# A_wo matmuls in a hardware loop with register addresses, the PE program not aligned to a block, filler matmuls written out

## Chip, cores, metric

One core of one Trainium2 chip (trn2). The metric is device time in microseconds (us), lower is better. The kernel is one decode step: an attention over a window of a key and value cache and a small gated feed-forward block, added up for a single token.

## The reference

```python
def reference(A_x, A_k_cache, A_v_cache, A_wq, A_wo, B_x, B_w_r, B_w_gate, B_w_up, B_w_down):
    x = A_x                                   # (1, 1, 512)
    xn = _layernorm(x)
    # A: 32 query heads on 8 key/value heads, the last 4096 places of the cache
    q = xn @ wq; p = softmax(q k^T / sqrt(128)); o = p v
    a = o.reshape(1, 1, 4096) @ wo            # A_wo: (4096, 512), bf16, 4 MB
    # B: one token, so it always is the chosen one
    y = (silu(xn @ w_gate) * (xn @ w_up)) @ w_down * sigmoid(xn @ w_r)
    return x + a + xn + y
```

(This is cut and put together from two functions; names as in the original.) All of it has to be read once: 30.7 MB of weights and cache for some 40 million multiply-adds. What matters here is the product with A_wo, (1 x 4096) by (4096 x 512): 32 matmuls with a contraction of 128 each.

## The kernel before

Every weight is loaded by one DMA queue in the order of use. A_wo comes in four transfers of 1 MB, one for 8 matmuls each, and w_down in five small ones behind it:

```python
    wo_chunks = [(0, 8), (8, 16), (16, 24), (24, 32)]
    t_wo = [dma(sy, f"wo{k}", wo_sb[:, j0 * D:j1 * D], wo_v[:, j0 * D:j1 * D]) for k, (j0, j1) in enumerate(wo_chunks)]
    wd_chunks = [(0, 4), (4, 8), (8, 11), (11, 13), (13, 14)]
```

The end of the program of TensorE (PE), all into one row of PSUM:

```python
    te.matmul(a_ps, lhsT=zst[:, 0:1], rhs=zmov[:], start=True, stop=False, skip_group_check=True)
    fill(F4)
    PE.need(t_oT2)
    for k, (j0, j1) in enumerate(wo_chunks):
        PE.need(t_wo[k])                      # wait for this quarter of A_wo
        for j in range(j0, j1):               # a Python loop: 32 matmuls written out
            te.matmul(a_ps, lhsT=oT2[:, j:j + 1], rhs=wo_sb[:, j * D:(j + 1) * D], start=False, stop=False, ...)
    PE.need(t_hT)
    for k, (j0, j1) in enumerate(wd_chunks):
        PE.need(t_wd[k])
        for j in range(j0, j1):
            ins = te.matmul(a_ps, lhsT=hTr[:, j, 0:1], rhs=wd_sb[:, j * D:(j + 1) * D], ...)
    ...                                       # + residual on VectorE (DVE), then the write of 1 KB
```

`fill(n)` emits a hardware loop of n passes with two matmuls of zeros; it keeps PE busy while it waits (L150 from 65.36 to 66.17 us, just ahead of A_wo). Hardware loops (`te.Fori`) also drive the keys (8 passes, 40 matmuls each) and the values (8 passes). A line at the start of PE's program, `te.addr_align(256, offset=0, max_nops=0)`, asks for a start at a multiple of 256 instructions; such a stretch is called a block below. In the records of the kernel before, a branch over the padding stands at 1.05 us (295 ns), and the instruction packets have 16 KB. How many instructions one packet holds is not shown.

Of the kernel before, what the change touches and what calls it, by code (L numbers as in the profile page):

```python
# [38 lines left out]
def kernel(  # L39
# [16 lines left out]
    D = A_x.shape[2]  # L56
# [10 lines left out]
    RJ = (HQ * DH) // P  # L67
# [30 lines left out]
    zst = sb("zst", [P, P], BF16)  # L98
    zmov = sb("zmov", [P, 512], BF16)
# [16 lines left out]
    oT2 = sb("oT2", [P, RJ], BF16)  # L116
# [8 lines left out]
    ps = nc.alloc_psum_tensor("ps", [P, 8, 512], F32)  # L125
# [6 lines left out]
    a_ps = ps[0:1, 5, :]  # L132
# [5 lines left out]
    wo_sb = k_flat[:, FB * D:(FB + RJ) * D]  # L138

    S = lambda n: nc.alloc_semaphore(n)  # L140
    PE, ACT, DVE, POOL, SP = (Eng(nc, nc.tensor, "pe"), Eng(nc, nc.scalar, "act"), Eng(nc, nc.vector, "dve"),
                              Eng(nc, nc.gpsimd, "pool"), Eng(nc, nc.sync, "sp"))
    te, ac, ve, gp, sy = nc.tensor, nc.scalar, nc.vector, nc.gpsimd, nc.sync

    def fill(n, k=2):
        if n <= 0:
            return
        with te.Fori(0, n):
            for _ in range(k):
                te.matmul(ps[:, 7, :], lhsT=zst[:], rhs=zmov[:], start=True, stop=True)  # L150

    def dma(eng, name, out_, in_):
        s = S("d_" + name)
        eng.dma_start(out=out_, in_=in_).then_inc(s, 16)  # L154
        return (s, 16)

    te.addr_align(256, offset=0, max_nops=0)
    t_x = dma(ac, "x", xrow[:], A_x.rearrange("a b d -> (a b) d"))
    t_wr = dma(ac, "wr", wr_row[:], B_w_r.rearrange("(a d) -> a d", a=1))
    wq_v = A_wq.rearrange("(p kt) n -> p kt n", kt=KT)  # L160
# [33 lines left out]
                                     op0=ALU.subtract, op1=ALU.mult))  # L194
    PE.need(t_zst, t_zmov)
    fill(W0)
    PE.need(t_xn, t_ident)
    for kt in range(KT):
        ins = te.matmul(ps[:, 6, 256 + kt:257 + kt], lhsT=xn_row[:].rearrange("a (p k) -> a k p", k=KT)[:, kt, :],  # L199
                        rhs=ident_bf[0:1, 0:1], start=True, stop=True)  # L200
# [22 lines left out]
    t_qe = []  # L223
    t_qpad = []
    fill(W1)
    for hf in range(2):
        if hf == 1:
            for ch in range(2):
                te.matmul(sc[:, ch, :], lhsT=zst[:], rhs=zmov[:], start=True, stop=False, skip_group_check=True)
            fill(WQ)  # L230
        PE.need(t_wq[hf], t_ps0)
        for kt in range(KT):
            for c in range(4):
                ins = te.matmul(ps[32 * c:32 * c + 1, hf, :], lhsT=xnT[:, kt:kt + 1],  # L234
                                rhs=wq_sb[:, kt, (4 * hf + c) * 512:(4 * hf + c + 1) * 512],
                                start=(kt == 0), stop=(kt == KT - 1), tile_position=(0, 32 * c))
        t_qp = PE.mark(ins)
        ACT.need(t_qp)
        t_qe.append(ACT.mark(ac.copy(out=q4[:, hf, :], in_=ps[:, hf, :])))  # L239
        if hf == 1:  # L240
            for _ in range(WK):
                te.matmul(ps[:, 7, :], lhsT=zst[:], rhs=zmov[:], start=True, stop=True)
        PE.need(t_qe[hf], t_gfb)
        if hf == 1:
            PE.need(t_qpad[0])
        for hl in range(4):
            ins = te.transpose(qT_ps[:, hl, :], q4[:, hf, hl * DH:(hl + 1) * DH], ident_bf[:])  # L247
        t_qt = PE.mark(ins)
        DVE.need(t_qt, t_qpad0)
        dst = bass.AP(qpad, (4 * hf) * 32 + 16 * hf, [[HKV * 32, P], [36, 4], [1, 4]])  # L250
        t_qpad.append(DVE.mark(ve.tensor_copy(out=dst, in_=qT_ps.rearrange("p h (c r) -> p c h r", r=32)[:, :, :, 0])))  # L251
# [72 lines left out]
    with te.Fori(1, 9) as i:  # L324
# [17 lines left out]
    t_wo = [dma(sy, f"wo{k}", wo_sb[:, j0 * D:j1 * D], wo_v[:, j0 * D:j1 * D]) for k, (j0, j1) in enumerate(wo_chunks)]  # L342
# [17 lines left out]
                              start=True, stop=True))  # L360
# [48 lines left out]
    with te.Fori(1, 9) as i:  # L409
# [4 lines left out]
        for tl in range(4):  # L414
            ins = te.matmul(pv_ps[32 * tl:32 * tl + 16, :], lhsT=pTcur[:, tl, :],  # L415
                            rhs=vin[:, 0].rearrange("p (q t) d -> p t q d", t=4)[:, tl],
                            start=True, stop=False, tile_position=(0, 32 * tl))
        ins.then_inc(pe_pva, 1)
        te.wait_ge(s_vb, i)
        for tl in range(4):  # L420
            ins = te.matmul(pv_ps[32 * tl:32 * tl + 16, :], lhsT=pTcur[:, 4 + tl, :],
                            rhs=vin[:, 1].rearrange("p (q t) d -> p t q d", t=4)[:, tl],
                            start=False, stop=True, tile_position=(0, 32 * tl))
# [18 lines left out]
    for m in range(2):  # L442
        PE.need(t_g if m == 0 else t_u)
        for kt in range(KT):
            for c in range(4):
                ins = te.matmul(ps[32 * c:32 * c + 1, 2 + m, 0:FC], lhsT=xnT[:, kt:kt + 1],
                                rhs=wgu[:, m * KT * F + kt * F + c * FC:m * KT * F + kt * F + (c + 1) * FC],
                                start=(kt == 0), stop=(kt == KT - 1), tile_position=(0, 32 * c))
# [14 lines left out]
    te.matmul(a_ps, lhsT=zst[:, 0:1], rhs=zmov[:], start=True, stop=False, skip_group_check=True)  # L463
    fill(F4)
    PE.need(t_oT2)
    for k, (j0, j1) in enumerate(wo_chunks):
        PE.need(t_wo[k])
        for j in range(j0, j1):
            te.matmul(a_ps, lhsT=oT2[:, j:j + 1], rhs=wo_sb[:, j * D:(j + 1) * D], start=False, stop=False, skip_group_check=True)  # L469
    PE.need(t_hT)  # L470
    for k, (j0, j1) in enumerate(wd_chunks):
        PE.need(t_wd[k])
        for j in range(j0, j1):
            ins = te.matmul(a_ps, lhsT=hTr[:, j, 0:1], rhs=wd_sb[:, j * D:(j + 1) * D], start=False, stop=(j == FB - 1),  # L474
                            skip_group_check=True)
# [36 lines left out]
```

## Time and profile before

83.44 us, median of 3 runs (83.2 to 83.69). Span in the profile: 81.6 us.

| what (profile or trace records of the kernel before) | value |
|---|---|
| moved from HBM | 30.67 MB, 376 GB/s over the span, some 420 in its middle |
| landing of the four quarters of A_wo (last of 16 engines) | 65.60, 68.47, 70.95, 73.44 us |
| last landing of w_down | 77.93 us |
| A_wo matmuls, start of the first, end of the last | 66.1 and 75.4 us |
| w_down matmuls end | 78.5 us |
| 16 KB instruction packets (queue 8) | at 2.1 and 65.5 us |

How to read it: each weight or cache transfer is split over 16 engines (16 semaphore updates in the records), and its landing is complete when the slowest engine has delivered its part (PE starts on the last quarter of A_wo at 73.48 us, 0.04 us after the last of the 16 updates and 1.6 us after the first). "Spread" below is the time from the first engine's semaphore update to the last one's. The views list PE's register, branch and wait instructions apart from its matmuls and weight loads, under PEldq; what carries them out is called PE's sequencer here, and the matmuls and weight loads that it has passed are called queued. That it runs ahead of the matmuls shows in the kernel before: the register instructions and branches of the last filler loop (L148) stand at 64.16 to 64.85 us, while the gate and up matmuls, which come earlier in the program, run until 64.78 us.

### The profile page before, as it was taken

The numbers are of one execution on the slowest core, as the hardware profiler recorded it, in microseconds if no ns is written. First come the engines' busy times: TensorE is split into PE (matmuls) and PEld (weight loads), VectorE is DVE, ScalarE is ACT, GpSimd is POOL, SyncE is SP. The second block draws the span as 40 slices with busy tenths as digits, with TensorE's granted clock in tenths as the row PEclk, the third lists the DMA queues.
The fourth block names the chain that finished last, engine by engine and source line by source line (L and its number), as shares of the span: only waits on it lengthen the run. The fifth ranks groups of instructions, "written<-read, shape, count | busy, mean of one in ns | idle before, by whom it ended". The sixth has DMA issues, their size and how long they took to land.

```text
span 81.6 us, 1567 instructions
## 1 busy us (share of the span) xinstructions
PE 60.0 (74%) x592; PEld 29.8 (37%) x596; DVE 43.5 (53%) x103; ACT 29.6 (36%) x40; POOL 7.3 (9%) x27
## 2 busy tenths in 40 slices
PE   0012267748999999999997776888878997779940
PEld 0012102117776685775862322223223432223200
DVE  3775000019586977977964479878880590000030
ACT  1940020020498696796863062223432200000000
POOL 5910001000121121211210000000000000000000
PEclk9999999999999999999999999999999999999999
DMA  0799999999999999999999999999999999999300
GB/s 1 203 416 424 420 408 428 426 414 442 402 438 410 426 426 418 434 406 438 402 426 426 418 430 410 474 393 422 443 443 385 426 410 430 408 408 395 139 0 1
DMA packets 4953, 30.72 MB, mean 376 GB/s; under 512 B 467, under 2 KB 598, under 8 KB 2134
## 3 DMA queue, kind: packets, MB, share of 16 engines
q1 hardware_dynamic: 4946, 30.67, 91.4%
q8 instruction: 2, 0.03, 0.2%
q14 instruction: 1, 0.01, 0.0%
q10 hardware_dynamic: 4, 0.00, 0.0%
HBM read 30.67 MB, written 0.00 MB: 376 GB/s over the span
## 4 chain that ended last, share of the span: by engine, by line
SPq 49%; DMA 39%; PE 6%; issue 2%; DVE 1%
SPq L154 49%; DMA k_sb<-in_A_wo_dram 39%; PE ps L474 4%; PE ps L469 2%; DVE res L478 1%; SPq L507 0%; SPq L74 0%
## 5 line engine op out<-in xcount | busy, mean ns | idle before, releaser
L283 ACT COPY kT<-ps 128x1024 bf16<-128x1024 bf16 x19 | 18.4, 1021 | 7.8 <-PE ps L309 7.8
L309 PE MATMUL ps<-ident_bf,kin 128*128 128x128 bf16 x256 | 18.2, 228 | 0.9 <-DVE kin L275 0.6
L309 PEld LDWEIGHTS ps<-ident_bf,kin 128*128 128x128 bf16 x256 | 15.4, 102 | 4.9 <-issue 4.0
L275 DVE COPY kin<-k_sb 128x1024 bf16<-128x1024 bf16 x32 | 12.2, 423 | 0.1
L280 DVE COPY kT<-ps 128x1024 bf16<-128x1024 bf16 x13 | 9.0, 692 | 4.4 <-PE ps L309 4.3
L469 PE MATMUL ps<-k_sb,oT 128*1 128x512 bf16 x32 | 7.5, 378 | 1.7 <-DMA k_sb<-in_A_wo_dram 1.7
L401 ACT CAST pvS<-ps 128x512 bf16<-128x512 f32 x8 | 4.7, 586 | 9.6 <-PE ps L406 9.6
L478 DVE TENSOR_TENSOR res<-ps,resid 1x512 bf16<-1x512 f32 x1 | 0.7, 678 | 11.2 <-PE ps L474 11.2
L382 DVE COPY vin<-v_sb 128x2048 bf16<-128x2048 bf16 x8 | 5.5, 685 | 1.5 <-PE ps L415 1.5
L234 PE MATMUL ps<-wq_sb,xnT 128*1 128x512 bf16 x32 | 3.8, 621 | 2.8 <-DMA wq_sb<-in_A_wq_dram 2.8
L251 DVE COPY qpad<-ps 128x16 bf16<-128x16 bf16 x2 | 0.3, 175 | 9.7 <-PE ps L247 9.7
L388 DVE COPY vin<-v_sb 128x2048 bf16<-128x2048 bf16 x8 | 5.5, 684 | 0.0
L415 PE MATMUL ps<-vin,pTcur 128*16 128x512 bf16 x32 | 3.1, 381 | 2.6 <-ACT pvS L401 2.2
L469 PEld LDWEIGHTS ps<-k_sb,oT 128*1 128x1 bf16 x32 | 2.3, 83 | 6.8 <-DMA k_sb<-in_A_wo_dram 3.2
L427 PE MATMUL ps<-zmov,zst 128*128 128x512 bf16 x16 | 4.7, 376 | 0.0
L317 PE MATMUL ps<-kT,qB 128*32 128x512 bf16 x36 | 4.2, 413 | 0.4 <-ACT kT L283 0.3
L239 ACT CAST q<-ps 128x512 bf16<-128x512 f32 x2 | 1.2, 586 | 9.0 <-PE ps L234 9.0
L317 PE MATMUL ps<-kT,qA 128*32 128x512 bf16 x32 | 4.2, 389 | 0.0
L266 POOL COPY qA<-qpad 128x32 bf16<-128x32 bf16 x8 | 2.1, 260 | 17.9 <-PE ps L317 9.1
L199 PE MATMUL ps<-ident_bf,xn_row 1*128 1x1 bf16 x4 | 0.3, 166 | 4.6 <-DVE xn_row L193 4.6
L150 PE MATMUL ps<-zmov,zst 128*128 128x512 bf16 x10 | 3.2, 381 | 0.4 <-issue 0.3
L268 POOL COPY qB<-qpad 128x32 bf16<-128x32 bf16 x8 | 1.9, 235 | 15.6 <-PE ps L317 15.6
(85 smaller groups left out, 51.8 us busy)
## 6 DMA issues: line engine op xcount, KB each, us to landing
k_sb<-in_A_k_cache_dram SPq DMA_DIRECT2D x8, 1024.0 KB, 20.7
v_sb<-in_A_v_cache_dram SPq DMA_DIRECT2D x8, 1024.0 KB, 27.1
wq_sb<-in_A_wq_dram SPq DMA_DIRECT2D x2, 2048.0 KB, 10.9
k_sb<-in_A_wo_dram SPq DMA_DIRECT2D x4, 1024.0 KB, 31.1
wq_sb<-in_B_w_gate_dram SPq DMA_DIRECT2D x1, 1792.0 KB, 27.9
wq_sb<-in_B_w_up_dram SPq DMA_DIRECT2D x1, 1792.0 KB, 30.0
k_sb<-in_B_w_down_dram SPq DMA_DIRECT2D x2, 512.0 KB, 30.3
k_sb<-in_B_w_down_dram SPq DMA_DIRECT2D x1, 384.0 KB, 26.1
```

Source lines behind the costliest of these rows:

```text
L154: eng.dma_start(out=out_, in_=in_).then_inc(s, 16)
L234: ins = te.matmul(ps[32 * c:32 * c + 1, hf, :], lhsT=xnT[:, kt:kt + 1], rhs=wq_sb[:, kt, (4 * hf + c) * 512:(4 * hf + c + 1) * 512], start ...
L275: ve.tensor_copy(out=kin[:, b, :], in_=k_sb[:, g, b, :]).then_inc(s_c[b], 1)
L280: ve.tensor_copy(out=kT[:, b, :], in_=tp[:, b, :]).then_inc(s_ev[b], 1)
L283: ac.copy(out=kT[:, b, :], in_=tp[:, b, :]).then_inc(s_ev[b], 1)
L309: ins = te.transpose(tp[:, b, k * P:(k + 1) * P], kin[:, b, k * P:(k + 1) * P], ident_bf[:])
L317: ins = te.matmul(sc[32 * cq:32 * cq + 32, ch, :], lhsT=q[:], rhs=kT[:, b, e * 512:(e + 1) * 512], start=False, stop=False, tile_position= ...
L382: ve.tensor_copy(out=vin[:, 0], in_=v_sb[:, g, 0:16, :]).then_inc(s_va, 1)
L388: ve.tensor_copy(out=vin[:, 1], in_=v_sb[:, g, 16:32, :]).then_inc(s_vb, 1)
L401: ac.copy(out=pvS[:].rearrange("p t d -> p (t d)"), in_=pv_ps).then_inc(s_pvs, 1)
L427: te.matmul(ps[:, 7, :], lhsT=zst[:], rhs=zmov[:], start=True, stop=True)
L469: te.matmul(a_ps, lhsT=oT2[:, j:j + 1], rhs=wo_sb[:, j * D:(j + 1) * D], start=False, stop=False, skip_group_check=True)
```

## The change

The intent, as I read it: make PE's program shorter, so that fewer blocks of instructions have to be fetched while the weights stream in. The written-out matmuls with A_wo become a loop of 16 passes; ScalarE (ACT) turns the four landings into a counter that the loop can wait for with its own index. The space gained is used to write the filler matmuls out, and the alignment goes.

```diff
-    def fill(n, k=2):
-        if n <= 0:
-            return
-        with te.Fori(0, n):
-            for _ in range(k):
-                te.matmul(ps[:, 7, :], lhsT=zst[:], rhs=zmov[:], start=True, stop=True)
+    def fill(n):
+        for _ in range(2 * n):
+            te.matmul(ps[:, 7, :], lhsT=zst[:], rhs=zmov[:], start=True, stop=True)
...
-    te.addr_align(256, offset=0, max_nops=0)
...
+    s_wo = S("s_wo")
     for k, (j0, j1) in enumerate(wo_chunks):
-        PE.need(t_wo[k])
-        for j in range(j0, j1):
-            te.matmul(a_ps, lhsT=oT2[:, j:j + 1], rhs=wo_sb[:, j * D:(j + 1) * D], start=False, stop=False, skip_group_check=True)
+        ACT.need(t_wo[k])
+        ac.sem_inc(s_wo, (j1 - j0) // 2)
+    with te.Fori(1, RJ // 2 + 1) as i:
+        te.wait_ge(s_wo, i)
+        for o in range(2):
+            te.matmul(a_ps, lhsT=oT2[:, bass.ds(i * 2 + (o - 2), 1)], rhs=wo_sb[:, bass.ds(i * (2 * D) + (o - 2) * D, D)],
+                      start=False, stop=False, skip_group_check=True)
```

## The prediction

> **What bounds the kernel now.** I read the page's slices first. The DMA row stands at 9 from the third slice to the 37th and the TensorE (PE) row falls only at its ends, so the weights' transfer from HBM sets the pace. The chain of waits, at its end, says what is added after the transfer:
>
> ```profile
> 41.85 31.59 DMA k_sb<-in_A_wo_dram
> 73.44 0.04 issue
> 73.48 1.89 PE ps L469 x8
> 75.37 3.12 PE ps L474 x14
> 78.49 0.02 issue
> 78.52 0.68 DVE res L478
> ```
>
> The columns are start, length, what. The last quarter of A_wo lands at 73.44 us, and from there everything is serial: its 8 matmuls (L469), the 14 with w_down (L474), the addition of the residual, then the write of the output. So all that makes PE finish later than 78.49 us comes out at the end one for one. The time line of PE alone shows the stage that the change rewrites:
>
> ```profile
> 66.10 1.89 PE L469 MATMUL ps<-k_sb,oT 128*1 128x512 bf16 x8
> 68.52 1.89 PE L469 MATMUL ps<-k_sb,oT 128*1 128x512 bf16 x8 [0.53 <-DMA k_sb<-in_A_wo_dram]
> 71.00 1.89 PE L469 MATMUL ps<-k_sb,oT 128*1 128x512 bf16 x8 [0.59 <-DMA k_sb<-in_A_wo_dram]
> 73.48 1.89 PE L469 MATMUL ps<-k_sb,oT 128*1 128x512 bf16 x8 [0.60 <-DMA k_sb<-in_A_wo_dram]
> 75.21 3.27 PE L474 MATMUL ps<-k_sb,hTr 128*1 128x512 bf16 x14
> ```
>
> A quarter of A_wo arrives every 2.48 us, PE needs 1.89 us for it (216 ns from one matmul's start to the next, in the records) and then waits some 0.6 us in brackets. The slack of this stage is thus 0.6 us in 2.48: two matmuls may take 0.62 us before PE, instead of the transfer, sets the pace. The changed kernel drives the same 32 matmuls by a hardware loop of 16 passes with two matmuls each, so the question is what one pass costs PE's sequencer. The kernel before has such a loop already, the one over the value blocks (L409), with register addresses in its small collecting matmuls (L406). The views of these two lines list what the sequencer itself executes there (duration min/median/max in ns, PEldq being its sequencer):
>
> ```profile
> L406 PEldq FUSED_REGOPS  x8: 64/64/73, 49.7 to 61.4; - x8
> L409 PEldq MOVE  x9: 29/37/38, 48.4 to 60.2; - x9
> L409 PEldq ALU_OP  x8: 36/36/36, 49.9 to 61.5; - x8
> L409 PEldq COMPARE_BRANCH  x8: 76/207/209, 50.0 to 61.6; - x8
> ```
>
> FUSED_REGOPS computes the addresses (several register operations in one instruction), MOVE copies the counter, ALU_OP increments it, and the branch goes back (207 ns) or falls through (76 ns).
>
> [...]the register instructions of the last filler loop (L148) run at 64.16 to 64.85 us while PE still works at the queued gate and up matmuls. [...]the page's instruction queue
>
> ```profile
> q8 instruction: 2, 0.03, 0.2%
> ```
>
> holds two packets of 16 KB, which the records put at 2.1 and 65.5 us. No stall shows in the loops before.
>
> **The change part by part.**
>
> *Pass of the new loop.* The built order shows in each pass: MOVE, FUSED_REGOPS with a wait against the counter, a second FUSED_REGOPS, weight load and matmul, a third FUSED_REGOPS, weight load and matmul, ALU_OP, branch. I take the spacing of starts from the records of the old loop at 51.39 us: FUSED_REGOPS to ALU_OP 141 ns (64 busy and 77 of hand-over, with twelve queued PE instructions in between, so a queued instruction with a register address costs nearly nothing there), ALU_OP to branch 102, taken branch to the next MOVE 268; MOVE to its successor is 97 at 48.49 us. The three FUSED_REGOPS of the new loop hold 6, 2 and 6 register operations against 5 in the old one. At an estimated 9 ns for an operation (one alone is 36 ns busy, five are 64, that is 7; I round up) they take 150, 110 and 150 ns. Sum: 97 + 150 + 110 + 150 + 102 + 268 = 877 ns; [...]**0.86 us a pass**, against 0.43 us of matmul in it and 0.62 us between the data for two passes' worth. The sequencer becomes the bound of this stage. It cannot run ahead of the data either, because its first FUSED_REGOPS waits for the counter of landed pieces.
>
> *When the loop ends.* It can start when oT2 is there (L453 ends at 65.12 us) and the first quarter has landed (65.60 us by its semaphore)[...]: 65.7 us. The pieces never hold it up again: after four passes it is at 69.1 (data 68.5), after eight at 72.6 (71.0), after twelve at 76.0 (73.5). Sixteen passes end at 65.7 + 16 x 0.86 = 79.5 us. The last branch falls through (130 ns less)[...]. All of w_down has landed by 77.93 us, so its 14 matmuls run at 216 ns: 13 x 0.216 + 0.38 = 3.2 us, PE ends at 82.7 instead of 78.49. **Added: 4.2 us**, all on the path. Nothing after it changes: residual 0.68 us, then the write.
>
> *Fillers written out.* The filler loops (14 matmuls of zeros) lose four MOVE, seven ALU_OP and seven branches. They stand in waits for VectorE (the softmax) or for A_wo, so what they save, up to 0.3 us each, was idle time. Zero, or a tenth or two in the softmax.
>
> *No alignment.* PE no longer jumps over padding at the start (a branch of 295 ns at 1.05 us); PE's first work waits for VectorE until 4.5 us anyway: zero. The program is some 60 instructions shorter in its A_wo part, so the block fetched at 65.5 us may fall away or move. That fetch matters a little today: one of the 16 DMA engines serves it, and the spread between the first and the last engine's landing grows from 1.18 us (gate, up and the first quarter) to 1.56 us from the next quarter on. Without it the last quarter would land up to 0.4 us earlier. That is a gain only where the transfer still is the bound, which by the sum above it no longer is.
>
> **The rivals.** (1) *A pass is short enough to hide*, under 0.62 us: then PE still waits for the pieces, and the end moves between -0.4 us (fetch gone) and +0.6 us (remainder of the last four passes). For it: queued instructions cost almost nothing, and the author chose the loop. Against: the branch, ALU_OP and MOVE alone are 467 ns, which leaves 150 for three FUSED_REGOPS of which each has 64 or so busy. 83 to 84 us; I give it one in twelve. (2) *PE loses its clock*: with two matmuls of 216 ns in 860 it is half busy, against three quarters in the old stage, [...]here the records show half clock only at 83.2 us, 4.8 us after the last matmul, and a window of about half load in the softmax didn't trigger it). Then the matmuls still fit into the pass (854 ns), but w_down's would take 427 ns: up to +3 us, 90 us. About one in ten. (3) *A loop now straddles a block of instructions* because nothing is aligned. The loop over the keys is some 85 instructions, the one over the values 33, the new one 10; the place in the block isn't visible to me. [...]if each pass fetches again, at 1 to 2 us a fetch as the two packets took, eight passes would add 10 us or more. One in fifteen, and the range doesn't cover it. (4) *The transfer hides it anyway*: no, since the slack at the end is under 2 us (w_down landed at 77.93, PE done at 78.49).
>
> **Range and chances.** 83.44 + 4.2 = 87.6 us. A pass of 0.79 us gives 86.5, one of 0.93 us 88.8, as 16 passes multiply each error. With the clock on the high side and a small gain from fetch and hop on the low side I take 85.7 to 90.0. Faster by over 2% (under 81.8) has no mechanism that I can size: 0.03. Within 2% is rival (1): 0.07. Slower: 0.90.
>
> **What would show it.** In the profile after, the loop's branch should have 16 records of some 208 ns, FUSED_REGOPS 48, and pass to pass 0.86 us; the matmuls of A_wo should come in pairs with "issue", not DMA, as what ended their idle time, from 66 to 79.5 us; the w_down matmuls should stand in a row without waits; the chain of waits should lead back over PE's sequencer to about 66 us instead of the DMA to 73.4. The softmax and the loops over keys and values should be where they were within 0.3 us. I am wrong if the A_wo matmuls still wait for the DMA (rival 1), if PE's clock row falls or w_down's matmuls are 427 ns apart (rival 2), or if the key loop has new gaps with instruction packets beside them (rival 3).

The forecast came to 0.86 us a pass, 82.7 us for PE's end and 87.6 us for the time, and three terms of that sum are 15 ns off the 877 ns of a pass, 0.1 us for the hop of the first landing through ACT (from 65.60 to 65.7 us), and a wait and a hand-over set off against the 130 ns of the last branch. All three were estimates without a trace behind them. The 427 ns of the second rival are in a trace: in the kernel before, two fillers (L229) start 427 ns apart at 12.68 and 13.10 us, and its records grant the full clock from 21.8 us on.

## The result, and the profile after

The changed kernel takes 88.72 us (median of 4 runs, 88.41 to 89.0) against 83.56 us of the kernel before on the same chip. The ratio is 1.0624, with a 95% interval of 1.0584 to 1.0664.

The end of the chain of waits of the changed kernel (start, length, what) answers to the chain shown in the prediction:

```profile
79.65 0.32 issue
79.97 0.59 PE ps L469 x2
80.56 3.12 PE ps L475 x14
83.70 0.68 DVE res L479
```

Where the chain before went back from the A_wo matmuls to a landing at 73.44 us, it now goes back through pairs of matmuls and "issue", which is time in which PE waited for nothing that the profile shows. The last landing of w_down is at 78.24 us and no longer matters; PE ends at 83.7 instead of 78.5 us. The time line of PE:

```profile
66.62 0.59 PE L469 MATMUL ps<-k_sb,oT 128*1 x2 [0.43 <-ACTq L465]
67.53 0.59 PE L469 MATMUL ps<-k_sb,oT 128*1 x2 [0.32 <-issue]
68.40 0.59 PE L469 MATMUL ps<-k_sb,oT 128*1 x2 [0.27 <-issue]
69.31 0.59 PE L469 MATMUL ps<-k_sb,oT 128*1 x2 [0.32 <-issue]
...
79.97 0.59 PE L469 MATMUL ps<-k_sb,oT 128*1 x2 [0.32 <-issue]
80.49 3.18 PE L475 MATMUL ps<-k_sb,hTr 128*1 128x512 bf16 x14
```

Two matmuls come every 0.87 or 0.91 us, in turn; only the first pair waited for data (ACTq is ACT's sequencer, which counts the landing: its first semaphore instruction is at 66.3 us and takes 17 ns). What fills the time between is in the views of the loop's two lines (min/median/max in ns):

```profile
L469 PEldq FUSED_REGOPS  x48: 42/74/84, 66.4 to 80.0; - x48
...
L466 PEldq MOVE  x17: 35/37/37, 65.2 to 79.6; - x17
L466 PEldq ALU_OP  x16: 36/36/36, 66.8 to 80.1; - x16
L466 PEldq COMPARE_BRANCH  x16: 76/208/208, 66.9 to 80.2; - x16
```

A pass has six control instructions: a MOVE, three FUSED_REGOPS, an ALU_OP and the branch. From start to start the first five cost the sequencer 95 to 198 ns each and the taken branch 266; their records are busy for only part of that. One more line of the page has changed:

```profile
q8 instruction: 1, 0.02, 0.1%
```

One 16 KB packet instead of two. The records put it at 45.4 us, and the first quarter of A_wo now lands at 66.31 us instead of 65.60.

### The profile page after: what moved, and what is told of

It reads as the page before. It is cut to its first block, busy times and chain, and to the rows that moved or that the text cites. A ratio compares the mean times of both kernels' runs of the same rounds, so it can differ in the third digit from the quotient of the medians.

```text
span 86.8 us, 1652 instructions
## 1 busy us (share of the span) xinstructions
PE 62.5 (72%) x596; PEld 29.9 (34%) x596; DVE 43.5 (50%) x103; ACT 29.7 (34%) x40; POOL 7.3 (8%) x27
## 4 chain that ended last, share of the span: by engine, by line
DMA 51%; PE 37%; issue 6%; DVE 1%; SPq 1%; ACT 1%; ACTq 0%
DMA k_sb<-in_A_wo_dram 37%; PE ps L305 14%; DMA wq_sb<-in_A_wq_dram 14%; PE ps L469 11%; PE ps L313 5%; PE ps L475 4%; PE ps L230 2%; DVE res L479 1%; SPq L151 1%; PE ps L243 1%; ACT q L235 1%; DVE kin L271 0%; DVE qpad L247 0%; SPq L508 0%; ACTq L465 0%
## 5 line engine op out<-in xcount | busy, mean ns | idle before, releaser
L469 PE MATMUL ps<-k_sb,oT 128*1 x32 | 9.5, 377 | 4.9 <-issue 4.5
L469 PEld LDWEIGHTS ps<-k_sb,oT 128*1 x32 | 2.5, 79 | 12.0 <-issue 10.7
L411 PE MATMUL ps<-vin,pTcur 128*16 128x512 bf16 x32 | 3.1, 381 | 2.6 <-ACT pvS L397 2.2
L423 PE MATMUL ps<-zmov,zst 128*128 128x512 bf16 x16 | 4.7, 377 | 0.0
L147 PE MATMUL ps<-zmov,zst 128*128 128x512 bf16 x14 | 3.7, 382 | 0.0
L417 PE MATMUL ps<-vin,pTcur 128*16 128x512 bf16 x32 | 3.1, 383 | 0.2 <-DVE vin L384 0.2
```

The source lines that it names most:

```text
L147: te.matmul(ps[:, 7, :], lhsT=zst[:], rhs=zmov[:], start=True, stop=True)
L423: te.matmul(ps[:, 7, :], lhsT=zst[:], rhs=zmov[:], start=True, stop=True)
L469: te.matmul(a_ps, lhsT=oT2[:, bass.ds(i * 2 + (o - 2), 1)], rhs=wo_sb[:, bass.ds(i * (2 * D) + (o - 2) * D, D)], start=False, stop=False, ...
```

## The experiments

Ten kernels were run. All gave results that the comparison with the reference accepts (experiment 6 shows that this says nothing of the A_wo product). "Pass" is the mean distance of the loop's branches.

### 1. The loop alone

The kernel before with the A_wo loop; alignment and filler loops kept.

```diff
+    s_wo = S("s_wo")
     for k, (j0, j1) in enumerate(wo_chunks):
-        PE.need(t_wo[k]) ... written-out matmuls
+        ACT.need(t_wo[k]); ac.sem_inc(s_wo, (j1 - j0) // 2)
+    with te.Fori(1, RJ // 2 + 1) as i:  ... as in the change
```

> The kernel before with the A_wo loop alone (aligned, filler loops kept). Theory S (PE's sequencer sets the pace: 16 passes of 0.89 us): pass spacing 0.89 us on average as in the changed kernel, ratio to before about 1.055; if the first A_wo quarter lands at 65.6 us as in the kernel before and not at 66.3, the end is some 0.7 us earlier than the changed kernel's. Rival L (the missing alignment or the written-out fillers make the loop slow, by its place in the instruction blocks): passes well under 0.89 us and a ratio near 1.00 to 1.02.

Measured: 88.0 us against 83.51, ratio 1.054 (1.0521 to 1.0559). The first quarter landed at 65.36 us, the pass was 0.888 us, PE ended at 82.70 us. The loop alone brings nearly all of the loss, also where the program is aligned; the 0.7 us to the changed kernel go with its later first landing (66.31 us).

### 2. Everything but the loop

The changed kernel with the 32 matmuls written out again.

```diff
-    with te.Fori(1, RJ // 2 + 1) as i: ...
+    for k, (j0, j1) in enumerate(wo_chunks):
+        PE.need(t_wo[k])
+        for j in range(j0, j1): te.matmul(a_ps, lhsT=oT2[:, j:j + 1], ...)
```

> The changed kernel with A_wo written out again (no alignment, fillers written out). Theory S: PE waits for the DMA again before each quarter of A_wo, ratio to before 1.00, or up to 1.01 if the instruction fetch at 45 us sets back a DMA engine and the last A_wo quarter lands 0.3 us or more later. Rival L: a good part of the 6.2% stays, ratio over 1.02.

Measured: 83.56 us against 83.51, ratio 1.0005 (0.9986 to 1.0023). The time line has the waits for the DMA back:

```profile
68.60 1.89 PE L465 MATMUL ps<-k_sb,oT 128*1 128x512 bf16 x8 [0.45 <-DMA k_sb<-in_A_wo_dram]
71.10 1.89 PE L465 MATMUL ps<-k_sb,oT 128*1 128x512 bf16 x8 [0.61 <-DMA k_sb<-in_A_wo_dram]
73.59 1.89 PE L465 MATMUL ps<-k_sb,oT 128*1 128x512 bf16 x8 [0.61 <-DMA k_sb<-in_A_wo_dram]
```

With the first experiment this settles the share of the parts: the loop is the loss, and alignment and fillers together cost nothing that can be measured as long as there is no loop.

### 3. No alignment alone

```diff
-    te.addr_align(256, offset=0, max_nops=0)
```

> The kernel before without the alignment alone. Theory S: ratio 1.00 within 0.01, no new gaps in the loops over keys and values. Theory F (a 16 KB instruction fetch sets one DMA engine back for good, and the layout decides when it comes): the fetch at 65.5 us moves, the one at 2.1 us goes away, and the spread between first and last engine of the A_wo landings changes by some 0.8 us with it; the time by at most that. Rival L: slower by over 2%.

Measured: 83.67 us against 83.51, ratio 1.0022 (0.9998 to 1.0047). The fetches moved, from 2.1 and 65.5 us to 46.7 and 76.5 us, and the spread of the first A_wo landing grew from 1.17 to 1.99 us, the size that theory F had. The trace has it grow in two steps: from 0.54 to 1.42 us at an instruction packet of 8 KB that theory F leaves out (queue 14, at 39.2 us; each run has one, at 37.7 to 40.4 us), and to 1.96 us at the 16 KB one. The last quarter landed at 73.74 instead of 73.44 us, PE ended at 78.74 instead of 78.48: 0.3 us between the two profiled executions. The medians differ by 0.16 us, which the interval does not tell from nothing. Against experiment 2 this also is the fillers' share: written out or looped, the two times lie 0.1 us apart, within their scatter.

### 4. Four matmuls a pass

```diff
-        ac.sem_inc(s_wo, (j1 - j0) // 2)
-    with te.Fori(1, RJ // 2 + 1) as i:
+        ac.sem_inc(s_wo, (j1 - j0) // 4)
+    with te.Fori(1, RJ // 4 + 1) as i:
         te.wait_ge(s_wo, i)
-        for o in range(2):
+        for o in range(4):      # addresses with i * 4, o - 4
```

> The changed kernel with 4 matmuls a pass, 8 passes. Theory S: a pass costs 0.89 us plus two address instructions of some 0.13 to 0.15 us, 1.15 to 1.19 us, under the 1.24 us in which four pieces of A_wo arrive: PE waits for the DMA again, ratio to before about 1.01 (0.5 us of pass remainder and the later landing). A rival that charges the loop as such (semaphore hop through ScalarE, register addresses on the matmuls themselves, a slower clock) keeps most of the 5 us: ratio 1.04 or more.

Measured: 84.25 us against 83.51, ratio 1.0089 (1.0072 to 1.0106).

```profile
67.55 1.02 PE L469 MATMUL ps<-k_sb,oT 128*1 x4 [0.15 <-issue]
68.82 1.02 PE L469 MATMUL ps<-k_sb,oT 128*1 x4 [0.25 <-ACTq L465]
70.04 1.02 PE L469 MATMUL ps<-k_sb,oT 128*1 x4 [0.20 <-issue]
71.33 1.02 PE L469 MATMUL ps<-k_sb,oT 128*1 x4 [0.27 <-ACTq L465]
```

Every second pass now waits for a landing (ACTq), so the stream sets the pace again: two passes take 2.49 us. Inside a quarter a pass takes 1.17 to 1.22 us, at the upper end of what was expected and just under the 1.24 us of the data. Loop, register addresses, the wait by register and the counter kept by ACT are all still there; with half the passes they cost 0.7 us instead of some 5.

### 5. One matmul a pass

The same edit with 1 in the place of 4: 32 passes. One look; its state is unknown.

> The changed kernel with one matmul a pass, 32 passes. Theory S: a pass has MOVE, one fused address instruction, one more register operation, weight load and matmul, ALU_OP, branch: 0.095 + 0.13 + 0.125 + 0.10 + 0.27 = 0.72 us, 32 passes 23 us from 66.4 us, so the A_wo matmuls end near 89.5 instead of 80.6 and the time is some 97.5 us. A rival that puts the 5 us down to the landing or the alignment expects no change from 88.7. PE is then 30% busy[...].

Measured: 98.12 us, span 96.1 us, pass 0.71 us, A_wo matmuls until 88.9 us. The loss follows the number of passes times their length, as expected. The clock did fall, in this one look; the clause in which the expectation left this open is cut. The page's row of the granted clock (40 slices of 2.4 us, tenths) and the time line:

```profile
PEclk9999999999999999999999999999965555555599
```

```profile
69.91 0.38 PE L469 MATMUL ps<-k_sb,oT 128*1 x1 [0.32 <-issue]
70.60 1.99 PE L469 MATMUL ps<-k_sb,oT 128*1 x3 [0.32 <-issue]
...
88.74 4.24 PE L475 MATMUL ps<-k_sb,hTr 128*1 128x512 bf16 x14
```

The records have half clock from 70.38 to 90.86 us, beginning 4 us after the loop's first matmul. Before that, PE's load was 0.216 us (the distance of two matmuls in a row) in a pass of 0.71 us, 30%; the view has no gap longer than 0.4 us, but the ends of matmuls in it are modelled, and by this load PE was idle for 0.5 us of a pass. The loop doesn't feel the fall, since a matmul of twice the length still fits into the pass (0.427 us of 0.71, which the passes keep). The first five of the w_down matmuls, 427 ns apart, do: 14 of them took 4.24 us, where they take 3.2 us at full clock.

### 6. The loop without addresses

```diff
-            te.matmul(a_ps, lhsT=oT2[:, bass.ds(i * 2 + (o - 2), 1)], rhs=wo_sb[:, bass.ds(i * (2 * D) + (o - 2) * D, D)],
+            te.matmul(a_ps, lhsT=oT2[:, o:o + 1], rhs=wo_sb[:, o * D:(o + 1) * D],
```

Its output is wrong, which doesn't matter for the time. (The comparison accepted it all the same: the attention's part of the output is too small for its tolerance, some 4e-5 beside values of about 1 when I compute it with random inputs of the reference's scales. So it says nothing of the A_wo product, here or in any other run.) One look; its state is unknown.

> The changed kernel with constant addresses in the loop (every pass multiplies pieces 0 and 1 again: the result is wrong on purpose, the work is the same). No fused address instructions: a pass is MOVE, ALU_OP, branch and the queued matmuls, 0.095 + 0.10 + 0.27 us, 0.46 to 0.52 us, under 0.62. Theory S in the form 'the register addresses push the pass over the limit': PE waits for the DMA again, time 83.5 to 84.2 us. If the branch alone were enough, or register-valued waits were slow, the time stays at 86 or more.

Measured: 83.69 us against a median of 83.49 for the kernel before in the same job; a pass takes 0.48 us.

```profile
65.95 2.06 PE L469 MATMUL ps<-k_sb,oT 128*1 128x512 bf16 x8
68.42 2.06 PE L469 MATMUL ps<-k_sb,oT 128*1 128x512 bf16 x8 [0.42 <-ACTq L465]
70.91 2.05 PE L469 MATMUL ps<-k_sb,oT 128*1 128x512 bf16 x8 [0.43 <-ACTq L465]
```

The four passes of a quarter take 2.05 us and then wait for the next. So neither the branch nor the wait by register breaks the change by itself: it is the three address instructions, 0.4 us a pass on top of 0.48, that carry the pass over the 0.62 us limit. By themselves they would fit too; the sum does not.

### 7. Eight matmuls a pass

Four passes, a quarter of A_wo each (the edit of experiment 4 with 8).

> The changed kernel with 8 matmuls a pass, 4 passes, one quarter of A_wo each. Theory S: a pass costs 0.89 + 6 x 0.14 = 1.7 us of sequencer time, under the 2.48 us in which a quarter lands and about the 1.73 us of its matmuls: ratio to before 1.00 to 1.01, not better than before.

Measured: 83.98 us against 83.49, ratio 1.0054 (1.0025 to 1.0083). The passes come every 2.49 us and their eight matmuls take 1.89 us, as when written out. PE ends 0.29 us later in the profile (78.77 instead of 78.48 us): 0.12 of it is the later landing of the last quarter (73.56 us), and the rest lies between that landing and PE's end (5.21 us instead of 5.04). The other 0.2 us of the loss isn't accounted for; the kernel before scatters by 0.4 us in this job.

### 8. The loop, aligned and shifted by 64 instructions

Experiment 1 with another place in the block:

```diff
-    te.addr_align(256, offset=0, max_nops=0)
+    te.addr_align(256, offset=64, max_nops=0)
```

> The aligned kernel with the loop of 2 (the first experiment) shifted by 64 instructions in its block. Theory F: the second 16 KB fetch comes earlier than 65 us, before the first quarter of A_wo has landed; that landing is then some 0.6 to 0.9 us later than the 65.4 us of the first experiment, the loop starts that much later and the time is 88.7 instead of 88.0 us (ratio 1.06 instead of 1.054), passes unchanged. If the fetch has nothing to do with it, the ratio stays 1.054.

Measured: 88.41 us against 83.49, ratio 1.0586 (1.0556 to 1.0617). The second fetch moved to 47.8 us, ahead of A_wo, and the first landing came 0.43 us later than in experiment 1, less than expected. Together with experiment 1 and the changed kernel:

| kernel | 16 KB fetches, us | first A_wo landing, us | pass, us | PE's end, us | ratio to before |
|---|---|---|---|---|---|
| loop alone | 2.1, 64.9 | 65.36 | 0.888 | 82.70 | 1.0540 |
| loop, shifted | 2.1, 47.8 | 65.79 | 0.874 | 82.96 | 1.0586 |
| the change | 45.4 | 66.31 | 0.887 | 83.67 | 1.0624 |

From the first landing to PE's end it is 17.2 to 17.4 us in all three, so the end follows this landing. In the changed kernel the fetch makes it late: the spread is 1.10 us in the last landing before the fetch, 1.94 in the first one after it and 2.02 in the first quarter of A_wo. In the shifted kernel the fetch does not: the last engine is 1.52 us behind the first before it and 1.51 in the first quarter, while another engine is set back to the same place (the second to last goes from 1.20 to 1.49 us; the trace does not name the engines, so this is read from the order of their 16 updates). So this experiment does not show what it was made for. Its spread is larger than that of experiment 1 from the first weights on (1.21 against 0.87 us) and grows to 1.52 at the 8 KB packet; why is open, and the intervals of the two ratios just touch.

### 9. A loop across a block border

The kernel before, aligned and shifted by 110 instructions.

```diff
-    te.addr_align(256, offset=0, max_nops=0)
+    te.addr_align(256, offset=110, max_nops=0)
```

> The kernel before, aligned but shifted by 110 instructions, so that by my count of the built program the loop over the keys (about instructions 102 to 187 of PE's program) lies across a 256-instruction border, at 212 to 297. The third rival of the prediction (a straddling loop fetches again in each pass) expects instruction packets in each of the eight passes and 10 us or more: over 93 us. [...]no such packets, the key loop's branches at the same times within 0.5 us, ratio 1.00 within 0.01.

The words cut are the condition of the other case, in which no pass fetches again.

Measured: 83.47 us against 83.36, ratio 0.9985 (0.9941 to 1.0029). One fetch came at 22.1 us and one at 72.4, none in the later passes of the key loop; its taken branches took 215 to 231 ns against 207 to 223 in the kernel before, and it ended 0.3 us earlier. Where the loader really put the loop is not visible in a trace, so this shows that the shift does no harm; that the loop lies across the border is my count. It also gives the cleanest size of a fetch: before 22 us all engines of a landing lie within 0.60 us, after it one lies 1.92 us behind the first and stays there to the end of the stream. That engine lost at least 1.3 and at most 1.9 us to one packet of 16 KB. The key loops of all twelve kernels agree: from the third pass on each pass takes 2.6 to 2.7 or 3.2 us whatever the layout. Only the second differs (3.6 to 4.8 us), and on the whole it is longer the later the records grant the full clock (at 20.6 us in the changed kernel, with 3.61 us for the pass; at 21.8 and 3.75 before; at 25.2 in experiment 10).

### 10. Another shift, in search of a gain

The same edit with an offset of 200.

> The kernel before, shifted by 200 instructions in its block: a search for a place in which no 16 KB fetch falls between the start and the last A_wo landing. Theory F: the time follows the last landings of A_wo, 82.9 to 83.9 us, a gain of at most 0.4 us where the last quarter lands by 73.1 us; where a fetch falls at 20 to 60 us, no gain.

Measured: 83.51 us against 83.36, ratio 0.9991 (0.9947 to 1.0035). The fetches came at 12.9 and 68.0 us and the last quarter landed at 73.70 us: no gain. No version tried beats the kernel before. Which instruction sets a fetch off could not be read from the traces and stays open.

## Why the prediction was right, point by point

- **The sequencer becomes the bound of the A_wo stage: right.** The view of the loop has the 48 address instructions and 16 branches that were foretold, "issue" in the place of the DMA, and w_down's matmuls in a row. Experiments 1 and 2 give the loss to the loop, 4, 5 and 7 show that it goes with the number of passes, and 6 that the address instructions carry it over the limit.
- **A pass of 0.86 us: 0.887 measured.** The single terms came out as 95 (MOVE, foretold 97), 132 and 125 (first and second address instruction, foretold 150 and 110), 173 on average (third to ALU_OP, foretold 150 less 15), 97 (ALU_OP, 102) and 266 ns (branch, 268). The term that was too small is the third: the deduction of 15 ns (an estimate without a trace) was wrong, and the distance is 153 or some 192 ns in turn. The extra 40 ns of every other pass is no property of this instruction: in experiment 1 it stands between ALU_OP and branch (96 or 136), in experiment 8 between the second and the third address instruction (120 or 160). Why is open. Sixteen times 0.027 is 0.43 us.
- **Start of the loop at 65.7 us: 66.38 measured, and this is the largest miss.** The step was "the block fetched at 65.5 us may fall away or move", taken as a gain or nothing. It moved to 45.4 us, ahead of A_wo, where the spread of the landings jumps from 1.10 to 1.94 us, and the first quarter came at 66.31 us, on which the loop's start depends. The hop through ACT, 0.07 us, was right (0.1 foretold, an estimate). Experiments 2 and 3, with fetches at 46.7 us, have the late landing too (66.07 and 66.28 us); experiment 8, meant to show this step, doesn't.
- **Sum.** PE's end was foretold as 82.7 us and came at 83.67: 0.68 from the landing and 0.43 from the passes, less some 0.14 where the last pass and the hand-over to w_down were shorter. The time, 88.72, lies in the range of 85.7 to 90.0, above its centre of 87.6. The room above the centre was meant for the clock and for a longer pass, not for a later landing, so that the range covers this part is luck.
- **Fillers and alignment cost nothing by themselves: right** (experiments 2 and 3, 1.0005 and 1.0022).
- **One sign was wrong, without a cost.** The softmax and the value loop should have stayed within 0.3 us of their place; they start 1.05 us earlier (44.23 instead of 45.28 us for the softmax). The fetch at 2.1 us is gone and the first keys land at 16.36 instead of 17.27 us; the rest is the second pass of the key loop (experiment 9). The A_wo stage does not gain from it, as it waits for the first quarter.
- **Sums and readings.** They come out, but for three small ones: one in twelve is 0.08, not 0.07; 87.6 plus 3 us is 90.6, not 90; and the softmax stretch called half loaded has PE busy in 3.81 of the 5.00 us from 44 to 49 us.
- **The rivals.** The hidden pass (1) did not come about with two matmuls a pass, but with eight it did, and nearly with four. The lost clock (2) did not occur at 49% load (0.432 of 0.887 us; the records have full clock from 20.6 to 88.9 us), but did at 30% in experiment 5 (one look); at which load it sets in is not shown. The straddling loop (3) didn't occur, and experiment 9 found no cost in a layout made for it. The stream did not hide the loss (4).

## What to carry to other kernels

In this kernel a hardware loop was nearly free only as long as the sequencer time of a pass stayed under the time in which its data arrived: 0.48 us of 0.62 in experiment 6 (one look), 1.17 to 1.22 of 1.24 in experiment 4 (0.7 us lost), but 0.887 against 0.62 in the change (5.2 us lost). So add up the distances from start to start of all control instructions (here 95 to 266 ns each, of which the busy records show about half), and put enough matmuls into a pass. Address computation was the part that decided it here; fewer passes with more matmuls each took the loss from 6.2% to 0.5%. While one stream of weights sets the pace, an instruction fetch is not always free either: in experiment 9 it set one DMA engine back by 1.3 to 1.9 us for the rest of the stream, and every later landing waited for that engine. In experiment 8 another engine was as late already, and the landings did not move.
